# Short expert jobs on raw fp32 weights, and an fp32 gate, in a fused attention and mixture-of-experts kernel

## The chip, the cores and the metric

The kernel runs on one core of a Trainium2 chip. The metric is the device time of one launch, in microseconds; lower is better. Engines are named as in the profile: PE is the matrix engine (TensorE; PEld its weight loads), DVE the vector engine, ACT the scalar engine, POOL GpSimd, SP the engine that issues most DMAs.

## The reference

Three parts follow one another: an attention over 1152 tokens (2 batches of 512 local and 64 global rows, 8 heads of 64), a dense expert layer, and a layer that sends each token to one of 8 experts. The change concerns the third, and the gate in front of it:

```
logits = x @ w_gate                       # x [1152, 512], w_gate [512, 8]
expert_idx = argmax(logits, axis=1)
gate_w = softmax(logits)[expert_idx]
# each expert takes its first 288 tokens, in order; the rest of them stay zero in the output
h = maximum(disp @ w1[e], 0)              # w1 [8, 512, 1024]
y = h @ w2[e]                             # w2 [8, 1024, 512]
out[i] = gate_w[i] * y[expert_idx[i], pos[i]]
```

All data is fp32. For the inputs that the reference makes, the experts get 197, 108, 0, 82, 696, 0, 5 and 0 tokens.

## The kernel before, in words

The attention and most of the dense layer fill the first 180 us. Then the dense layer's output product is made in four windows of 256, 288, 256 and 288 token columns (`moe_second`, L689). Products that need fp32 accuracy are made from splits: a value is stored as a rounded fp32r part and the fp32r remainder, and three fp32r products (high by high, high by low, low by high) stand for one.

**The gate.** For each window, `moe_second` copies each of four 128-row chunks of x out of PSUM (ACT, L714), splits it (DVE, L715 and L716), and multiplies both halves by `wgs`, in which the gate's weights and their remainders stand side by side, padded to 128 columns (two products a chunk, L699: a pair). `gate_weights` (L637) makes `wgs` once. `tail_logits` (L728) copies the 16 rows of the result, `lt`, to SBUF (L734, or L1090 for the last window), and small products with `dup8` (`ptl`, L738) turn them over and add the two halves; the copies to `L` (L740) begin the routing. For window 3, the last pair stands outside the loop, behind the transposes of job 0's last tokens (`xp`, L803), and ahead of job 0's first layer.

**The jobs.** The experts are ranked by count; job 0 is the largest, and empty ones come last. `first_wide` and `second` run job 0; while they do, `final` (L1101) and what it calls compute the routing of all tokens and the tile `order` (L1140), which holds each job's expert and count. Jobs 1 to 8 are each a `unit` of 128 tokens (`job`, L981), with two more units under branches (L988, L990) for jobs above 128 and 256. A unit costs the same for any number of tokens up to 128. First layer (L887): tokens are stationary, the weights move, 512 columns at a time, 24 products; relu to `hs` (L892), transposes (L908) and splits to `hhl` (L909, L910); second layer (L921), 24 products; scaling by the gate's value (L927) and an indirect DMA that scatters the rows to the output (L928). Beside it run, at places given by step counts: the splits of the next job's raw weights (`split`, ACT L828 and DVE L829), each followed by the load of the job after that into the raw buffer (L822, L824; from job 2 on under a condition, the count); the gather of tokens (L791) and their transposes and splits (`xprep`, L799). Raw weights stand in eight buffers of 128x1024 (`raw2`). The jobs are nested: behind each job a branch on the next count (L1164) goes on or jumps past all the code that is left.

**What sets the order.** `drive` (L760) runs a main generator, one step per product, and starts its sides when their step is due: a side's `yield n` means that its next piece comes n steps later. The pieces stand in that order in each engine's program; an engine works its program in order, and waits on others by semaphores.

## Time and profile before

| | us |
|---|---|
| median of 3 runs (345.7 to 345.88) | 345.73 |
| the profiled execution | 347.64 |
| its span, first to last instruction | 345.86 |
| attention, dense layer, windows 0 to 3 (to the start of job 0's first layer) | 239.8 |
| job 0, first and second layer | 239.8 to 272.4 |
| job 1 (two units) | 272.4 to 298.7 |
| job 2 | 298.7 to 311.8 |
| job 3 | 311.8 to 324.9 |
| job 4 | 324.9 to 338.4 |
| landing of the last output and closing | 338.4 to 345.9 |

PE is busy 325.7 us, 94% of the span; DVE 73%, ACT 54%, POOL 41%. The mean granted clock of PE is 0.98. Times in a timeline count from the span's start. In a row, the number behind `x` is how many instructions were put together, and square brackets hold the idle time of that engine just before and who ended it; matmul records overlap, so the pace is read from the next start and not from their length.

### The profile page before, as it was taken

How to read it: one execution, taken by the hardware profiler on the slowest of the kernel's cores; microseconds unless marked ns; L12 is line 12 of the kernel's file. 1: busy time of each engine (PE TensorE's matmuls, PEld its weight loads, DVE VectorE, ACT ScalarE, POOL GpSimd, SP SyncE). 2: the span in 40 equal slices, each digit the busy share in tenths (PEclk: the TensorE clock that was granted, in tenths of full speed). 3: DMA queues.
4: the chain of work that ended last, by engine and by line, in shares of the span. 5: the costliest groups of instructions: out<-in, count | busy, mean ns of one | idle time of the engine just before them, and what ended most of it. 6: DMA issues, size and time to landing. Idle time of an engine off the chain costs nothing. (4 is left out here: it accounts for less than half of the span.)

```text
span 345.9 us, 8542 instructions
## 1 busy us (share of the span) xinstructions
PE 325.7 (94%) x3119; PEld 271.1 (78%) x3119; DVE 251.0 (73%) x662; ACT 185.1 (54%) x461; POOL 141.5 (41%) x168
## 2 busy tenths in 40 slices
PE   7989779999998999999999999999999999999990
PEld 2444547777787899999999999998987778777780
DVE  1777979985879448998993327867997893387881
ACT  3975666866675232423441223355525892488890
POOL 0375678664557517757784000310005542111211
PEclk9998987999999999999999999999999999999998
DMA  7975669490427913133300033665397999187100
GB/s 244 411 258 205 218 227 329 167 336 12 148 110 210 185 55 123 67 117 123 122 2 0 2 121 137 215 214 193 127 395 261 341 323 341 62 293 252 53 30 15
DMA packets 26293, 60.91 MB, mean 176 GB/s; under 512 B 3019, under 2 KB 8139, under 8 KB 26240
## 3 DMA queue, kind: packets, MB, share of 16 engines
q1 hardware_dynamic: 24640, 55.69, 46.8%
q0 software_dynamic: 1600, 4.54, 4.1%
q8 instruction: 30, 0.49, 0.6%
q14 instruction: 23, 0.19, 0.2%
HBM read 61.64 MB, written 7.47 MB: 200 GB/s over the span
## 5 line engine op out<-in xcount | busy, mean ns | idle before, releaser
L426 PE MATMUL h<-xh,wh 128*128 128x256 f32 (+1 forms) x288 | 84.6, 294 | 0.4 <-DVE hA L413 0.4
L426 PE MATMUL h<-xl,wh 128*128 128x256 f32 (+1 forms) x288 | 84.7, 294 | 0.0
L426 PE MATMUL h<-xh,wl 128*128 128x256 f32 (+1 forms) x288 | 84.3, 293 | 0.0
L426 PEld LDWEIGHTS h<-xl,wh 128*128 128x128 f32 x288 | 55.1, 191 | 0.9 <-issue 0.7
L426 PEld LDWEIGHTS h<-xh,wh 128*128 128x128 f32 x288 | 54.9, 191 | 1.1 <-DVE hA L413 0.6
L426 PEld LDWEIGHTS h<-xh,wl 128*128 128x128 f32 x288 | 55.0, 191 | 0.3 <-issue 0.2
L416 POOL TENSOR_TENSOR hTl<-hA,hTh 128x256 fp32r<-128x256 f32 (+1 forms) x24 | 19.3, 802 | 58.0 <-ACT hTh L415 57.1
L791 POOL DMA_INDIRECT xg<-x2d,idsall x12 | 14.6, 1220 | 60.8 <-DMA rawb<-in_w_dram 33.3
L829 DVE TENSOR_TENSOR w1l<-rawb,w1h 128x1024 fp32r<-128x1024 f32 x20 | 24.0, 1226 | 11.6 <-ACT w1h L828 11.6
L921 PE MATMUL py<-w2h,hhl 128*128 128x512 f32 x112 | 29.7, 395 | 0.0
L415 ACT CAST hTh<-hA 128x256 fp32r<-128x256 f32 (+1 forms) x24 | 10.0, 418 | 35.2 <-DVE hA L413 35.2
L829 DVE TENSOR_TENSOR w2l<-rawb,w2h 128x1024 fp32r<-128x1024 f32 x23 | 27.4, 1218 | 1.9 <-ACT w2h L828 1.8
L226 POOL CAST xh<-xs 128x128 fp32r<-128x128 f32 x32 | 13.1, 409 | 37.7 <-ACT xs L224 37.7
L708 PE MATMUL x<-hTl,wo_h 128*128 128x256 f32 (+1 forms) x96 | 28.2, 294 | 0.0
L708 PE MATMUL x<-hTh,wo_l 128*128 128x256 f32 (+1 forms) x96 | 27.9, 291 | 0.2 <-POOL wo_l L328 0.2
L708 PE MATMUL x<-hTh,wo_h 128*128 128x256 f32 (+1 forms) x96 | 27.8, 290 | 0.0
L188 ACT ACTIVATE sm<-sm,nm 128x128 f32<-128x128 f32 x64 | 25.2, 399 | 4.7 <-DVE nm L183 4.6
L327 POOL TENSOR_TENSOR ct<-ct,wh 128x512 f32<-128x512 f32 x18 | 25.6, 1420 | 1.5 <-DVE ca L324 1.5
L413 DVE TENSOR_TENSOR hA<-hA,h 128x256 f32<-128x256 f32 (+1 forms) x48 | 20.7, 431 | 7.2 <-PE h L426 6.5
L328 POOL TENSOR_TENSOR wl<-ct,ca 128x512 fp32r<-128x512 f32 x18 | 23.9, 1329 | 2.9 <-DVE ca L326 1.6
L921 PEld LDWEIGHTS py<-w2h,hhl 128*128 128x128 f32 x112 | 20.9, 188 | 4.5
L183 DVE CUSTOM_DVE_ANT_0 sm<-s,mask 128x128 f32<-128x128 f32 x64 | 15.9, 285 | 10.4 <-PE s L171 10.0
(213 smaller groups left out, 767.3 us busy)
## 6 DMA issues: line engine op xcount, KB each, us to landing
rawb<-in_w_dram SPq DMA_DIRECT2D x51, 512.0 KB
raww<-in_w_dram SPq DMA_DIRECT2D x18, 512.0 KB
rawv<-in_v_dram SPq DMA_DIRECT2D x16, 512.0 KB
qk<-in_qk_dram SPq DMA_DIRECT2D x16, 320.0 KB
rawo<-in_w_out_dram SPq DMA_DIRECT2D x6, 512.0 KB
rw<-in_w_dram SPq DMA_DIRECT2D x5, 512.0 KB
out_dram<-zero SPq DMA_DIRECT2D x1, 2176.0 KB
rawg<-in_vo_dram SPq DMA_DIRECT2D x4, 512.0 KB
```

Source lines behind the costliest of these rows:

```text
L183: nc.vector.tensor_tensor_reduce(sm[:, j], ps[:, j, 0:P], mk, scale=-0.125, scalar=3.0e38, op0=ALU.add, op1=ALU.min, accum_out=nm[:, j : j ...
L188: nc.scalar.activation(sm[:, j], sm[:, j], AF.Exp, bias=nm[:, j : j + 1], scale=-1.0, accum_out=ssum[:, j : j + 1])
L226: nc.gpsimd.tensor_copy(dst[0], xs)
L327: nc.gpsimd.tensor_tensor(tf, tf, hi.bitcast(F32), op=ALU.subtract)
L328: nc.gpsimd.tensor_tensor(lo, tf, b.bitcast(F32), op=ALU.add)
L413: nc.vector.tensor_tensor(hA[:, :T], hA[:, :T], ph[:, :T], op=ALU.max)
L416: nc.gpsimd.tensor_tensor(hl[:, f_, c0 : c0 + T], hA[:, :T], dst.bitcast(F32), op=ALU.subtract)
L426: nc.tensor.matmul(ph[:, :T], lhsT=w_[:, a], rhs=x_[:, c, c0 : c0 + T], start=n == 0, stop=n == 11)
L708: nc.tensor.matmul(po[:, :T], lhsT=w_[:, f, d * P : (d + 1) * P], rhs=h_[:, f_, c0 : c0 + T], start=k == 0, stop=k == 17)
L791: nc.gpsimd.indirect_dma_start(out=xg[t], out_offset=None, in_=src, in_offset=bass.IndirectOffsetOnAxis(ap=IDS[j][0:n, t, 0:1].bitcast(I32 ...
L829: nc.vector.tensor_tensor(l_, raw_of(j, k), h_.bitcast(F32), op=ALU.subtract)
L921: nc.tensor.matmul(py[0:nt], lhsT=a[:, c, a0 : a0 + nt], rhs=w_[:, c], start=i == 0, stop=i == 23)
```

## The change

There are two parts. **Small jobs.** From job 2 on, a job of at most 32 tokens runs through `small` (L979 on). It takes the tokens unsplit (`XS`, a copy of 32 columns that `xprep` now makes) and the raw fp32 weights out of the eight raw buffers. In the first layer, 32 token columns are stationary and a quarter of the 1024 hidden columns moves in each of four column groups of PE: 4 x 4 products of 256 columns into one PSUM tile, groups in turn. Relu is shared by ACT and DVE, two transposes make the hidden part stationary, and the second layer is 2 x 4 x 4 products of 128 columns, a quarter of the output columns in each group. Four scalings put the quarters beside one another in `ys`. The branch between jobs now compares with 32, then with 0; the code of `small` stands first and the longer job's in the Else. Since the small job's weights are not split, what follows one isn't loaded by the usual path: `order` gets two more rows, the counts by which loads are done, and what is left over; jobs left over run in `rest`, at the end, one after the other. With the counts above, only job 4 is small, and nothing is left over. Job 3 still makes the splits of job 4's weights and its split tokens.

**Gate.** The gate's products are fp32 by fp32 in the same form: `wg` is padded to 32 columns, chunk d of x goes to column group d, four products a window in place of eight, and the four partial sums are added by the `dup8` product, which now contracts over 128 rows. The splits of x, `wgs`, `gate_weights` and the products inside the loop go. In window 3 the products move into `first_wide`, at its step 5, and `ptl` follows 8 steps later.

```diff
@@ -112,7 +112,7 @@
     ident = cst[:, 0:P]
-    dup8 = cst[0:16, 256:264]
+    dup8 = cst[:, 256:264]
@@ -134,6 +134,8 @@
     ones_b = const.tile([P, P], BF16, name="ones_b")
+    wg = const.tile([P, 4, 32], F32, name="wg")
+    nc.gpsimd.memset(wg, 0.0)
...
     def routing_start():
@@ -630,14 +632,7 @@
-    wg = s2.tile([P, 4, NE], F32, name="wg")
-    nc.sync.dma_start(wg, w_gate.rearrange("(c p) e -> p c e", p=P))
-    wgs = s2.tile([P, 4, P], F32R, name="wgs")
-    def gate_weights():
-        nc.vector.tensor_copy(wgs, zero.unsqueeze(1).to_broadcast([P, 4, P]))
-        nc.vector.tensor_copy(wgs[:, :, 0:NE], wg)
-        nc.vector.tensor_tensor(wgs[:, :, NE : 2 * NE], wg, wgs[:, :, 0:NE].bitcast(F32), op=ALU.subtract)
+    nc.sync.dma_start(wg[:, :, 0:NE], w_gate.rearrange("(c p) e -> p c e", p=P))
@@ -648,8 +643,6 @@
                     take(ws, 1)
-                if k == 100:
-                    gate_weights()
@@ -663,15 +656,13 @@
                 s2b.tile([P, 4, 288], F32, tag="x2T", name=f"x2T{wi}"),
-                [s2b.tile([P, 288], F32R, tag="x2hl", bufs=4, name=f"x2hl{wi}{i}") for i in range(4)],
-                s2b.tile([16, 288], F32, tag="lt", name=f"lt{wi}"),
+                s2b.tile([P, 288], F32, tag="lt", name=f"lt{wi}"),
...
             rawb[:, a : a + 288 * 4].rearrange("p (d c) -> p d c", d=4),
-            x2hl,
-            rawb[0:16, 288 * (8 + wi - 2) : 288 * (9 + wi - 2)],
+            rawb[:, 288 * (8 + wi - 2) : 288 * (9 + wi - 2)],
@@ -691,13 +682,6 @@
         x2T = XB[wi][0]
-        pl_ = ps_y.tile([P, 512], F32, tag="py", name=f"pl{c0}")
-        x2 = {}
-        def logits(d):
-            for k, x_ in enumerate(x2[d]):
-                nc.tensor.matmul(pl_[:, :T], lhsT=wgs[:, d], rhs=x_[:, :T], start=d == 0 and k == 0, stop=d == 3 and k == 1)
@@ -709,15 +693,9 @@
                         yield
-            x2h, x2l = XB[wi][1][2 * (d % 2) : 2 * (d % 2) + 2]
-            x2[d] = (x2h, x2l)
             nc.scalar.copy(x2T[:, d, :T], po[:, :T])
-            nc.vector.tensor_copy(x2h[:, :T], x2T[:, d, :T])
-            nc.vector.tensor_tensor(x2l[:, :T], x2T[:, d, :T], x2h[:, :T].bitcast(F32), op=ALU.subtract)
-            if d:
-                logits(d - 1)
             yield
-        TAIL.append((c0, T, x2T, pl_, logits))
+        TAIL.append((c0, T, x2T))
@@ -727,11 +705,12 @@
     def tail_logits(wi):
-        c0, T, x2T, pl_, logits = TAIL[wi]
-        lt = XB[wi][2]
-        if wi < 3:
-            logits(3)
-            nc.vector.tensor_copy(lt[:, :T], pl_[0:16, :T])
+        c0, T, x2T = TAIL[wi]
+        lt = XB[wi][1]
+        pl_ = ps_y.tile([P, 512], F32, tag="py", name=f"pl{c0}")
+        for d in range(4):
+            nc.tensor.matmul(pl_[32 * d : 32 * d + 32, :T], lhsT=wg[:, d], rhs=x2T[:, d, :T], start=True, stop=True)
+        nc.vector.tensor_copy(lt[:, :T], pl_[:, :T])
@@ -741,12 +720,12 @@
     def tail_rows(wi):
-        c0, T, x2T, pl_, logits = TAIL[wi]
+        c0, T, x2T = TAIL[wi]
...
                 nc.tensor.transpose(pt[0:n, d], x2T[:, d, c - c0 : c - c0 + n], ident)
-            xs = XB[wi][3][i]
+            xs = XB[wi][2][i]
@@ -804,6 +783,10 @@
         nc.vector.tensor_tensor(l_, pt[:, :, 0:nt], h_.bitcast(F32), op=ALU.subtract)
+        if j > 1 and t == 0:
+            nc.vector.tensor_copy(XS[0], pt[:, :, 0:32])
+    XS = []
     def hl_of(j, k):
@@ -814,10 +797,11 @@
-    def load(j, k):
+    def load(j, k, kw=None):
         if j < NJ:
-            kw = {} if j < 2 else {"cond": nsp[j] > 0}
+            if kw is None:
+                kw = {} if j < 2 else {"cond": nsp[j] > 0}
@@ -990,11 +974,70 @@
+    SMALL = 32
+    def small(j):
+        sx = pB.tile([P, 512], F32, tag="hs", bufs=2, name="sx")
+        sh = pB.tile([P, 512], F32, tag="hs", bufs=2, name="sh")
+        xs = XS[0]
+        ph = ACC[0][0]
+        for k in range(4):
+            for g in range(4):
+                r = slice(32 * g, 32 * g + 32)
+                nc.tensor.matmul(ph[r, 0:256], lhsT=xs[:, k], rhs=raw_of(j, k)[:, 256 * g : 256 * g + 256], start=k == 0, stop=k == 3)
+        hr = sx[:, P : P + 256]
+        hT_ = sh[:, 0:256].rearrange("p (i t) -> p i t", i=2)
+        pt = ps_x.tile([P, 2, P], F32, tag="px", name="st")
+        for i in range(2):
+            s_ = slice(i * P, i * P + P)
+            if i == 0:
+                nc.scalar.activation(hr[:, s_], ph[:, s_], AF.Relu)
+            else:
+                nc.vector.tensor_scalar_max(hr[:, s_], ph[:, s_], 0.0)
+        for i in range(2):
+            nc.tensor.transpose(pt[:, i], hr[:, i * P : i * P + P], ident)
+            if i == 0:
+                nc.scalar.copy(hT_[:, i], pt[:, i])
+            else:
+                nc.vector.tensor_copy(hT_[:, i], pt[:, i])
+        py = ps_y.tile([P, P], F32, tag="py", name="sy")
+        for i in range(2):
+            for k in range(4):
+                for q in range(4):
+                    r = slice(32 * q, 32 * q + 32)
+                    nc.tensor.matmul(py[r], lhsT=hT_[:, i, 32 * k : 32 * k + 32], rhs=raw_of(j, 4 + k)[:, i, q * P : q * P + P], start=i == 0 and k == 0, stop=i == 1 and k == 3)
+        i_ = IDS[j][0:32, 0]
+        y = pB.tile([P, DM], F32, tag="y", bufs=2, name="ys")
+        for q in range(4):
+            if q:
+                nc.scalar.mul(y[0:32, q * P : q * P + P], py[32 * q : 32 * q + 32], i_[:, 2:3])
+            else:
+                nc.vector.tensor_scalar(y[0:32, 0:P], py[0:32], i_[:, 2:3], None, op0=ALU.mult)
+        nc.gpsimd.indirect_dma_start(
+            out=out, out_offset=bass.IndirectOffsetOnAxis(ap=i_[:, 1:2].bitcast(I32), axis=0),
+            in_=y[0:32], in_offset=None, bounds_check=NT - 1, oob_is_err=False)
+    def value(i, j, top, **kw):
+        _, (r,) = nc.values_load_multi_w_load_instructions(order[0:1, i, j - 1 : j], min_val=0, max_val=top, **kw)
+        return r
+    def rest():
+        for j in range(3, NJ):
+            with tc.If(value(3, j, NT) > 0):
+                ereg[j] = value(0, j, NE - 1, engines=(mybir.EngineType.SP,))
+                for k in range(8):
+                    load(j, k, {})
+                gather_tile(j, 0)
+                xprep(j, 0, ps_x, "px")
+                small(j)
...
     wv0 = rt.tile([P, 1, NE], F32, name="wv0")
-    ereg, nreg, nsp = [None] * NJ, [None] * NJ, [None] * NJ
+    ereg, nreg, nsp, nrest = [None] * NJ, [None] * NJ, [None] * NJ, [None] * NJ
...
     def early():
@@ -1045,7 +1088,6 @@
     raw2 = [rawb[:, i * F2 : (i + 1) * F2] for i in range(NR)]
-    x2hl = [pA.tile([P, 288], F32R, name=f"x2hl{i}") for i in range(4)]
@@ -1086,23 +1128,23 @@
     )
-    TAIL[3][4](3)
-    nc.vector.tensor_copy(XB[3][2], TAIL[3][3][0:16, :288])
...
     xT[1] = pB.tile([P, 2, 4, CAP], F32R, name="xT1")
-    order = rt.tile([P, 2, NE], I32, name="order")
-    Y0, Y1, Y2, Y3, Y4 = 10, 12, 44, 12, 3
+    XS.append(pB.tile([P, 4, 32], F32, name="x32"))
+    order = rt.tile([P, 4, NE], I32, name="order")
+    Y0, Y1, Y2, Y3, Y4 = 10, 12, 40, 12, 3
     def final():
...
         rows_1(As[0], columns(0, 5), 5)
+        yield 4
@@ -1133,10 +1175,14 @@
         nc.vector.tensor_tensor(g_, r_.unsqueeze(1).to_broadcast([P, NE, NE]), eidx.unsqueeze(2).to_broadcast([P, NE, NE]), op=ALU.is_equal)
-        o_ = rt.tile([P, 2, NE], F32, tag="ordf", name="ordf")
+        o_ = rt.tile([P, 4, NE], F32, tag="ordf", name="ordf")
...
             nc.vector.tensor_reduce(o_[:, i], p_, axis=AX.X, op=ALU.add)
+        nc.vector.tensor_copy(o_[:, 2, 0:2], o_[:, 1, 0:2])
+        nc.vector.scalar_tensor_tensor(o_[:, 2, 2:NE], o_[:, 1, 1 : NE - 1], float(SMALL), o_[:, 1, 2:NE], op0=ALU.is_gt, op1=ALU.mult)
+        nc.vector.tensor_tensor(o_[:, 3], o_[:, 1], o_[:, 2], op=ALU.subtract)
+        nc.vector.tensor_reduce(o_[:, 3, 0:1], o_[:, 3, 2:NE], axis=AX.X, op=ALU.max)
@@ -1144,7 +1190,7 @@
         if a < b:
-            for i, (to, top) in enumerate(((ereg, NE - 1), (nsp, NT))):
+            for i, to, top in ((0, ereg, NE - 1), (2, nsp, NT)):
...
     def count_of(j):
@@ -1161,7 +1207,10 @@
         if j + 1 < NJ:
-            with tc.If(nreg[j + 1] > 0) if j > 1 else ExitStack():
+            with tc.If(nreg[j + 1] <= SMALL) as c:
+                with tc.If(nreg[j + 1] > 0):
+                    small(j + 1)
+            with c.Else():
@@ -1171,7 +1220,10 @@
     accumulators()
+    more_ = value(3, 1, NT)
     jobs(1)
+    with tc.If(more_ > 0, preferred_fallthrough_block=False):
+        rest()
@@ -1225,7 +1277,7 @@
     dup = np.zeros((P, NE))
-    dup[np.arange(16), np.arange(16) % 8] = 1.0
+    dup[np.arange(P), np.arange(P) % 32 % NE] = np.arange(P) % 32 < NE
```

In PE's program, where window 3 ends and `first_wide` begins (`xp` transposes job 0's last tokens, `ph` is `first_wide`'s first layer, `px` and `ptl` belong to the gate's tail). Before:

```order
L708 MATMUL x_3800<-hTh_2506,wo_l 128x288
L699 MATMUL pl_3698<-x2hl_3519,wgs 128x288
L699 MATMUL pl_3698<-x2hl_3520,wgs 128x288
L803 MATMUL xp_3838<-cst,xg_3525 128x32 x4
L699 MATMUL pl_3698<-x2hl_3521,wgs 128x288
L699 MATMUL pl_3698<-x2hl_3522,wgs 128x288
L866 MATMUL ph<-xT_3526,w1h_3527 128x288 x4
L866 MATMUL ph<-xT_3526,w1l_3528 128x288 x3
L748 MATMUL px_3883<-cst,rawb 32x128 x4
L866 MATMUL ph<-xT_3526,w1l_3528 128x288
L866 MATMUL ph<-xT_3526,w1h_3527 128x288
L738 MATMUL ptl_3892<-cst,rawb 32x8
```

The last pair stands between `xp` and `ph`, and `ptl` behind nine products of `ph`. In PE's program after the change, the same place:

```order
L692 MATMUL x_3738<-hTh_2508,wo_l 128x288
L782 MATMUL xp_3772<-cst,xg_3486 128x32 x4
L850 MATMUL ph<-xT_3487,w1h_3488 128x288 x4
L850 MATMUL ph<-xT_3487,w1l_3489 128x288
L712 MATMUL pl_3813<-rawb,wg 32x288 x4
L850 MATMUL ph<-xT_3487,w1l_3489 128x288 x2
L727 MATMUL px_3821<-cst,rawb 32x128 x4
L850 MATMUL ph<-xT_3487,w1l_3489 128x288
L850 MATMUL ph<-xT_3487,w1h_3488 128x288 x5
L717 MATMUL ptl_3838<-cst,rawb 32x8
```

No pair is left, the four fp32 products stand behind five products of `ph`, and `ptl` behind thirteen.

In DVE's program, the same place (`pct` to `col_all` and `sc` are routing, `w2l` a split of job 0's weights, `L` the copy of `ptl`). Before:

```order
L716 TENSOR_TENSOR x2hl_3522<-rawb,x2hl_3521 128x288
L806 TENSOR_TENSOR xT_3526<-xp_3838,xT_3526 128x4x32
L1090 COPY rawb<-pl_3698 16x288
L486 TENSOR_SCALAR pct<-pos_all 128x5
L487 SCALAR_TENSOR_TENSOR pct<-pos_all,pct 128x5
L488 SCALAR_TENSOR_TENSOR pcm<-pct,pos_all 128x5
L490 TENSOR_SCALAR col_all<-pos_all 128x5
L491 TENSOR_TENSOR col_all<-col_all,pct 128x5
L496 TENSOR_TENSOR sc_3864<-iota_b,pcm 128x640
L829 TENSOR_TENSOR w2l_3530<-rawb,w2h_3529 128x1024
L740 COPY L<-ptl_3892 32x8
```

The copy of the logits (`rawb<-pl`) comes first, ahead of the routing and the split. In DVE's program after the change, the same place:

```order
L785 TENSOR_TENSOR xT_3487<-xp_3772,xT_3487 128x4x32
L488 TENSOR_SCALAR pct<-pos_all 128x5
L489 SCALAR_TENSOR_TENSOR pct<-pos_all,pct 128x5
L490 SCALAR_TENSOR_TENSOR pcm<-pct,pos_all 128x5
L492 TENSOR_SCALAR col_all<-pos_all 128x5
L493 TENSOR_TENSOR col_all<-col_all,pct 128x5
L498 TENSOR_TENSOR sc_3796<-iota_b,pcm 128x640
L813 TENSOR_TENSOR w2l_3491<-rawb,w2h_3490 128x1024
L713 COPY rawb<-pl_3813 128x288
L855 SCALAR_TENSOR_TENSOR hhl<-ph,hhl 128x256
L857 SCALAR_TENSOR_TENSOR hhl<-ph,hhl 128x32
L719 COPY L<-ptl_3838 32x8
```

The copy now stands behind the split, and a piece of `first_wide`'s hidden layer (`hhl`) ahead of `L`.

In PE's program, from job 3 to job 4 (`acc` is a unit's first layer; `st` and `sy` are the transposes and the second layer of `small`). Before:

```order
L921 MATMUL py<-w2l_3858,hhl 32x512 x4
L921 MATMUL py<-w2h_3857,hhl 32x512 x4
L990 UNCONDITIONAL_BRANCH x2
L988 UNCONDITIONAL_BRANCH
L1164 COMPARE_AND_BRANCH
L887 MATMUL acc_4349<-w1h_3527,xT_3526 128x512 x4
L887 MATMUL acc_4349<-w1l_3528,xT_3526 128x512 x3
```

The longer job's first layer follows the branch directly. In PE's program after the change, the same place:

```order
L905 MATMUL py<-w2l_3789,hhl 32x512 x4
L905 MATMUL py<-w2h_3788,hhl 32x512 x4
L974 UNCONDITIONAL_BRANCH x2
L972 UNCONDITIONAL_BRANCH
L1210 COMPARE_AND_BRANCH
L1211 COMPARE_AND_BRANCH
L988 MATMUL acc_4291<-rawb,x_3791 32x256 x16
L999 MATMUL st<-cst,sx 128x128 x2
L1009 MATMUL sy<-rawb,sh 32x128 x32
L1211 UNCONDITIONAL_BRANCH x2
L871 MATMUL acc_4291<-w1h_3488,xT_3487 128x512 x4
```

The 50 products of `small` stand between the branch and the longer job, which a longer job jumps over; the same stands from job 1 to 2 and from job 2 to 3.

## Rows read from the trace of the kernel before

**Rows 1.** Busy us by stage: window, length, five engines, granted clock, DMA share, GB/s.

```profile
238.20:255.60 17.40, 17.00 (x135) 15.80 (x134) 15.55 (x61) 7.92 (x16) 0.00 (x0) 1.00 0.51 181
...
272.40:285.90 13.50, 13.50 (x70) 10.62 (x69) 13.06 (x16) 12.57 (x18) 6.55 (x6) 1.00 0.96 350
...
324.85:338.44 13.59, 12.80 (x60) 10.03 (x60) 11.79 (x12) 11.57 (x15) 2.34 (x2) 1.00 0.11 35
338.44:345.90 7.46, 0.00 (x0) 0.00 (x0) 0.44 (x1) 0.00 (x0) 1.05 (x1) 0.77 0.05 12
```

**Rows 2.** Timeline of the last job: start, duration, engine, line, operation, shapes, idle time before.

```profile
324.86 1.19 PE L887 MATMUL acc<-w1h,xT 128*128 128x512 f32 x4 [0.32 <-PEq L988]
...
325.60 1.12 POOL L928 DMA_INDIRECT out_dram<-y,idsall  x1 [3.44 <-ACTq L988]
...
336.57 1.09 PE L921 MATMUL py<-w2h,hhl 128*128 128x512 f32 x4
337.75 0.69 ACT L927 ACTIVATE y<-py,idsall 128x512 f32<-128x512 f32 x1 [0.59 <-ACT w2h L828]
338.71 1.05 POOL L928 DMA_INDIRECT out_dram<-y,idsall  x1 [3.52 <-ACTq L988]
```

**Rows 3.** Timeline, TensorE in the attention: fp32 products, one at a time, then in column groups.

```profile
31.27 0.75 PE L240 MATMUL sgp<-qk,qg 128*64 128x320 f32 x2
...
61.22 0.43 PE L213 MATMUL pv<-rawv,ph 128*32 128x64 f32 x16
...
69.96 0.65 PE L277 MATMUL gpv<-rawg,gph 128*32 128x64 f32 x32
```

**Rows 4.** Landing of output writes: the one issued at 325.60, then all five together.

```profile
DMA to landing us min/median/max: 4.3/4.3/4.3
...
DMA to landing us min/median/max: 2.6/4.3/7.8
```

**Rows 5.** Timeline, TensorE: a pair of gate products in window 0, and what follows it.

```profile
189.30 0.40 PE L699 MATMUL pl<-x2hl,wgs 128*128 128x256 f32 x2
189.53 0.28 PE L708 MATMUL x<-hTh,wo_h 128*128 128x256 f32 x1
```

**Rows 6.** Timeline, end of window 3 and start of job 0, TensorE, VectorE and ScalarE.

```profile
238.20 0.42 PE L699 MATMUL pl<-x2hl,wgs 128*128 128x288 f32 x2
...
238.55 0.43 PE L803 MATMUL xp<-cst,xg 32*128 32x32 f32 x4
...
239.02 0.27 ACT L805 CAST xT<-xp 128x128 fp32r<-128x128 f32 x1 [0.22 <-PE xp L803]
...
239.20 0.89 PE L699 MATMUL pl<-x2hl,wgs 128*128 128x288 f32 x2 [0.21 <-DVE x2hl L715]
239.55 0.28 DVE L806 TENSOR_TENSOR xT<-xp,xT 128x128 fp32r<-128x128 f32 x1
...
239.80 0.59 PEld L866 LDWEIGHTS ph<-xT,w1h 128*128 128x128 f32 x4
...
240.13 0.45 DVE L1090 COPY rawb<-pl 16x288 f32<-16x288 f32 x1 [0.29 <-PE pl L699]
...
241.64 0.76 PE L738 MATMUL ptl<-cst,rawb 16*32 16x8 f32 x6
241.98 1.22 DVE L829 TENSOR_TENSOR w2l<-rawb,w2h 128x1024 fp32r<-128x1024 f32 x1
```

**Rows 7.** Timeline, VectorE: the cast of the job order, and the splits behind it.

```profile
259.96 0.42 DVE L1140 CAST order<-ordf 128x16 int32<-128x16 f32 x1
...
263.67 3.53 DVE L829 TENSOR_TENSOR w1l<-rawb,w1h 128x1024 fp32r<-128x1024 f32 x3 [2.40 <-ACT w1h L828]
```

**Rows 8.** Jumps over two units (L988) on TensorE: count, ns min/median/max, starts.

```profile
L988 PEldq COMPARE_BRANCH  x3: 313/318/318, 308.8 to 334.9; - x3
```

**Rows 9.** Branches of L1164 to the next job on TensorE, and ScalarE's last waits, same columns.

```profile
L1164 PEldq COMPARE_BRANCH  x4: 70/132/3445, 311.7 to 341.7; - x4
...
L1164 ACTq EVENT_SEMAPHORE  x2: 17/17/17, 341.3 to 341.4; - x2
```

## The prediction

> **What bounds the kernel now.** I read the busy times by stage first, then the timeline of the last job, then the timeline where the gate's last window meets job 0. In the stages of job 0 and of job 1's first unit, TensorE is busy 17.0 of 17.4 and 13.5 of 13.5 us at a granted clock of 1.00, its upper level, 2.4 GHz [rows 1]; so a product removed there shortens the chain and a wait added to TensorE lengthens it. The reference's inputs put 197, 108, 0, 82, 696, 0, 5 and 0 tokens on the experts: jobs of 288 (capped), 197, 108, 82 and 5 tokens. Only the last, job 4, is at most 32. It takes a whole job's 13.59 us [rows 1] for 5 tokens: TensorE from 324.86, the scaling at 337.75, the output write at 338.71, then 7.15 us of landing and closing to 345.86 with no engine at work [rows 2]. What moves that write's issue moves the end.
>
> **Job 4, products.** The changed form multiplies fp32 by fp32 with 32 stationary columns. One fp32 product is two records; of the one with 320 columns the two take 0.75 us and one alone 0.48 on average, so a pass costs 0.27 us, 0.84 ns a column, and about 0.22 us to drain [rows 3]. In four column groups 16 records of 64 columns take 0.43 and 32 take 0.65 [rows 3]: 16 more cost 0.22, where 16 x 64 x 0.84 ns one after another is 0.86. The four groups run at once. The Trainium skill, "TensorE: Matmul & The Clock Gate", section "Part 3: Packing small matmuls — row/col tiling", speaks against a full factor: 3.07 times with four row tiles, 2.38 with three column tiles; as an estimate at 3.07 the new products would cost 1.6 us more and the time would be 340.3. These rows say four, though no row shows it at 128 or 256 columns, so the row decides for the forecast.
>
> The first layer is 32 records of 256 columns: 32 x 256 x 0.84 ns / 4 + 0.22 = 1.94 us. The second is 64 of 128 columns, 1.94 too. Between them stand relu, two transposes and a copy. ScalarE and VectorE take 0.27 and 0.28 for 128x128 out of PSUM; four small transposes take 0.43 [rows 6], so two are taken as 0.3. With 0.15 of handing over that is 1.0 us. Two branches that are not taken stand where one did, at 0.07 [rows 9]. So TensorE starts at 324.95, ends layer one at 326.9, starts layer two at 327.9 and is done at 329.85.
>
> **Job 4, output.** The new y is the buffer of job 3's y, whose write was issued at 325.60 [rows 2] and landed 4.3 us later [rows 4], at 329.9: a tie. Three scalings on ScalarE at 0.27 give 330.75. The write follows a scaling's end by 0.27 (337.75 + 0.69 to 338.71) [rows 2], so it is issued at 331.05, **7.66 us earlier**. Landing and closing follow as before. But TensorE's jump over the unused jobs, which takes 3.45 us now [rows 9], is followed by one over the code for what is left over: 329.9 + 3.45 + 0.1 + 3.45 = 336.9. ScalarE's last wait stands at 341.3, 2.9 us after its scaling [rows 2, 9], so twice that gives 336.6. The closing needs them by about 337.2, hence both stay hidden; POOL's own extra jump I put at **+0.3** (0 to 2). Removed with job 4's old form are ScalarE's and VectorE's splits for an empty job 5; nothing waits for them.
>
> **Gate.** A pair of gate products occupies 0.23 us to the next start [rows 5]: four are 0.94 in a window of 256 and 1.05 in one of 288. Four fp32 products in column groups are 0.43 us of passes plus part of the drain, 0.55 (0.43 to 0.65), or 0.62 at 288. Windows 0 to 2 gain 0.39 + 0.43 + 0.39 = 1.2. Window 3 loses two pairs on the chain, 0.53; the third hides under the wait for job 0's tokens. The last pair, which waited for VectorE's split, goes: first_wide's loads start at 239.80 [rows 6], and without it when ScalarE's copy is done, 239.02 + 0.27, so 0.45 earlier. Against that, the products come back inside first_wide at 0.62. And ptl, 9 steps into first_wide now, stands at step 13; its input, the lt copy, stands on VectorE behind xT, five small ops, sc and a whole split of 1.22 (in the trace: 240.13 for the copy, the split at 241.98 behind it) [rows 6]. That stretch moves 0.6 earlier, so the split ends about 242.4 and the copy (0.45) at 242.85, while TensorE arrives about 242.1: a stall with the hand-over of 0.85 (0 to 1.2). Behind the wait are first_wide's own products. Sum: -1.2 - 0.53 - 0.45 + 0.62 + 0.85 = **-0.7** (-1.6 to +0.3). VectorE also drops the splits of x2; TensorE was not waiting for those of windows 0 to 2.
>
> **Order of the jobs.** VectorE gets four small ops before the cast to order, each at most that cast's 0.42: at most 1.7, and 2.40 us of idle time stand a few rows later [rows 7]. The weight loads of job 2 go out that much later ahead of a stage where DMA is 0.96 busy [rows 1]; I take 0 and keep 0.5. The copy of 32 columns per job to XS is at most the 0.28 of a 128x128 one; in job 1's first unit VectorE has 13.06 of 13.5 us filled [rows 1], in the others more room: nothing, at most 0.3. One more register load, once: +0.1 (0 to 0.3).
>
> **Branches.** From job 1 to 2 and from 2 to 3 the branch falls through now, 0.07 us [rows 9], and will be taken, over small's code. TensorE's jump over two units takes 0.32 [rows 8]; small has 50 products, the two units 112, so this is the nearest row, and the far end is the 3.45 of the last jump [rows 9]. I take 0.45 each, since it stands directly behind a jump of the other kind: **+0.9** with the extra compare (0.2 to 6.9).
>
> **Sum.** -7.66 + 0.3 - 0.7 + 0.1 + 0.9 = -7.0 us in a span of 345.86. The profiled execution took 347.64; the median of the runs is 345.73, and the difference carries over: **338.7 us**.
>
> **Rivals.** *Jumps into code that is not there.* For it: the last jump's 3.45 [rows 9]; against it: 0.32 three times [rows 8]. One of the two at 3.45 gives 341.7, both 344.7, and with a closing that TensorE's second far jump prolongs by up to 2 us, 346.7. The Trainium skill, "Runtime: NRT & Kernel Launch", section "Instruction fetch mechanics", says that a taken branch out of the two pages held waits for a fetch; by that the 3.45 is a far target, and the new jumps depend on where a page ends.
>
> *Job 3's write lands late.* All five landings reach from 2.6 to 7.8 us [rows 4]. At 7.8 the scaling waits until 333.4 instead of 329.9: 342.2.
>
> *The gate goes to an end of its range.* No gain: 339.4; no stall at ptl: 337.8.
>
> *The groups overlap in part.* From the shorter row with its drain, 0.86 / 0.43 = 2.0 [rows 3]. Serial, job 4's products are 13.7 us and the gate's 7.3; at 2.0 this costs 3.0 and 1.3 us more than taken: 343.0.
>
> *The groups do not overlap at these widths* (slower than before). Then job 4 costs 10.2 and the gate 5.0 us more: 354. It turns to slower below an overlap of 21 / (5.25 + 7.0) = 1.7. Against it stand both rows of four groups.
>
> *The change doesn't do what it says*: the fourth count is above 32 and the branches alone stay: -0.7 + 0.1 + 1.4 + 0.1, 346.6. Against it: five units of output after job 0, and the 5 tokens.
>
> **How the numbers follow.** Forecast 0.60; one far jump 0.09; both 0.05 (of it 0.02 faster, 0.02 same, 0.01 slower); late landing 0.08; gate 0.08; part overlap 0.05; no overlap 0.03; no small job 0.02. Faster by over 0.2% (0.7 us, about what a measurement of this kernel can tell from no change): 0.92, same 0.02, slower 0.06. The low end is the forecast with the gate at -1.6, branches at 0.2 and no extra jump of POOL: 336.8. The high end takes in the landing and one far jump: 342.2.
>
> **What would show it.** In job 4: the first layer's records (L988 of the changed kernel) in under 2.1 us and the second's (L1009) too, the scaling starting at once, or idle with the earlier write as its cause; the write at about 7 us ahead of the old. In first_wide: an idle stretch of TensorE ahead of ptl with the lt copy as releaser. At 1 to 2 and 2 to 3: branches on TensorE of 0.3 rather than 3 us. After the last write: closing of some 7.4 us. The prediction is wrong if TensorE's gaps between jobs grow by over 1 us each, or if the groups' records follow one another.

## The result, and the profile after

The changed kernel takes 343.01 us (median of 22 runs, against 346.95 for 22 runs of the kernel before); the ratio is 0.988, 95% interval 0.986 to 0.991. Two of its runs, at 346.28 and 432.46 us, were over 1.5% above its fastest, and the ratio leaves them out. The changed kernel is 3.9 us faster where 7.0 were forecast, and its median lies outside the range of 336.8 to 342.2. The forecast started from 345.73, and the kernel before takes 1.2 us more in these runs; on the forecast's base the gain gives 341.8. The profiled execution has a span of 342.68 us.

Spans don't compare well here: the attention, whose code is nearly the same in all these kernels, ended up to 3.3 us apart from one profiled execution to the next (first product of window 0 at 179.4 to 182.7 us). So I compare from that product on, stage by stage, each from its first TensorE product to that of the next (differences of starts in the timelines; the last two stages are cut at the issue of the last output write). The columns to the right are experiments told of below.

| stage, us | before | after | gate only | shifted back | no rest |
|---|---|---|---|---|---|
| windows 0 to 3 | 57.78 | 54.54 | 54.58 | 54.54 | 54.54 |
| job 0, first layer | 15.67 | 16.23 | 16.23 | 16.24 | 16.32 |
| job 0, second layer | 16.87 | 17.09 | 16.87 | 17.06 | 16.81 |
| job 1, first unit | 13.68 | 13.69 | 13.68 | 13.67 | 13.72 |
| job 1, second unit, to job 2 | 12.56 | 12.84 | 12.56 | 12.96 | 12.96 |
| job 2, to job 3 | 13.13 | 16.41 | 13.13 | 13.28 | 13.28 |
| job 3, to job 4 | 13.03 | 14.76 | 13.03 | 13.31 | 13.31 |
| job 4, to the issue of its output | 13.85 | 7.20 | 13.85 | 7.20 | 7.22 |
| landing and closing | 7.15 | 7.27 | 7.31 | 8.45 | 4.00 |
| sum | 163.7 | 160.0 | 161.2 | 156.7 | 152.2 |

Two things moved by more than they should, in opposite directions: the windows gained 3.2 us, and jobs 2 and 3 lost 5.0 between them.

**Between jobs 2 and 3.** TensorE's three branches to the next job in the kernel after (count, ns as min/median/max, first and last start), the answer to [rows 9]:

```profile
L1210 PEldq COMPARE_BRANCH  x3: 72/219/3350, 296.8 to 327.8; - x3
```

The one from job 1 to 2 takes 0.22 us, the one from 3 to 4, not taken, 0.07; the one from 2 to 3 takes 3.35. The timeline of TensorE there:

```profile
308.76 1.10 PE L905 MATMUL py<-w2h,hhl 128*128 128x512 f32 x4
313.45 2.07 PE L871 MATMUL acc<-w1h,xT 128*128 128x512 f32 x4 [3.60 <-ACT w1h L812]
315.32 1.73 PE L871 MATMUL acc<-w1l,xT 128*128 128x512 f32 x4
```

The last group of job 2 starts at 308.76 and its products end at 309.85; job 3 starts 3.60 later. The row blames ScalarE's w1h, whose last split for job 3 had ended at 303.77:

```profile
302.72 1.05 ACT L812 CAST w1h<-rawb 128x1024 fp32r<-128x1024 f32 x1
```

And job 3's first products come slowly: four take 1.87 to the next start, where the same four of job 2 take 1.04. The busy times (columns as in [rows 1]) of job 2's first products and of job 3's:

```profile
297.04:300.20 3.16, 3.16 (x14) 2.58 (x15) 1.57 (x2) 2.02 (x4) 1.00 (x1) 1.00 0.14 50
313.45:317.82 4.37, 4.37 (x13) 3.48 (x13) 0.94 (x1) 0.00 (x0) 0.00 (x0) 0.63 0.88 335
```

Behind the 3.6 us of idling, TensorE's granted clock is 0.63 on average over 4.37 us, between its two levels of 1.2 and 2.4 GHz; job 2's stretch ran at 1.00. Job 3's thirteenth product from its start is followed after 4.60 us, job 2's after 3.12: 1.5 us lost.

**The gate's place.** The timeline that answers to [rows 6]:

```profile
236.87 0.27 ACT L784 CAST xT<-xp 128x128 fp32r<-128x128 f32 x1
...
237.19 0.79 PE L850 MATMUL ph<-xT,w1h 128*128 128x288 f32 x4 [0.35 <-ACT xT L784]
...
238.04 0.69 PE L712 MATMUL pl<-rawb,wg 128*32 128x288 f32 x8
...
238.66 0.54 PE L850 MATMUL ph<-xT,w1l 128*128 128x288 f32 x2
238.87 1.22 DVE L813 TENSOR_TENSOR w2l<-rawb,w2h 128x1024 fp32r<-128x1024 f32 x1
...
240.00 0.45 DVE L713 COPY rawb<-pl 128x288 f32<-128x288 f32 x1
...
240.51 0.68 PEld L717 LDWEIGHTS ptl<-cst,rawb 128*32 128x32 f32 x6 [0.31 <-DVE rawb L713]
```

job 0's first layer starts 0.05 after ScalarE's copy; the four fp32 products take 0.62 to the next start; the copy of the logits starts behind the split, and ptl's weights wait 0.31 us for it.

**Job 4**, answering to [rows 2]:

```profile
328.21 1.93 PE L988 MATMUL acc<-rawb,x 128*32 128x256 f32 x32 [0.56 <-DVE w2l L813]
...
330.29 0.28 ACT L995 ACTIVATE sx<-acc 128x128 f32<-128x128 f32 x1 [1.86 <-PE acc L988]
...
330.62 0.33 PE L999 MATMUL st<-cst,sx 128*128 128x128 f32 x1 [0.47 <-ACT sx L995]
330.67 0.29 DVE L997 TENSOR_SCALAR sx<-acc 128x128 f32<-128x128 f32 x1 [1.52 <-ACT sx L995]
330.98 0.27 ACT L1001 COPY sh<-st 128x128 f32<-128x128 f32 x1 [0.42 <-PE st L999]
...
331.30 0.33 PE L999 MATMUL st<-cst,sx 128*128 128x128 f32 x1 [0.36 <-ACT sh L1001]
...
331.56 1.95 PE L1009 MATMUL sy<-rawb,sh 128*32 128x128 f32 x64
...
333.58 0.34 DVE L1016 TENSOR_SCALAR ys<-sy,idsall 32x128 f32<-32x128 f32 x1 [1.62 <-PE sy L1009]
334.00 1.14 ACT L1014 ACTIVATE ys<-sy,idsall 32x128 f32<-32x128 f32 x3 [2.76 <-DVE ys L1016]
335.42 0.89 POOL L1017 DMA_INDIRECT out_dram<-ys,idsall  x1 [5.39 <-POOLq L1210]
```

The two layers take 1.93 and 1.95 us. In between, VectorE's relu starts when ScalarE's has ended, and the second transpose when ScalarE's copy has; ScalarE's scalings start when VectorE's has ended. The write goes out 7.20 us after the start, in place of 13.85.

### The profile page after: what moved, and what is told of

Its sections match the earlier page's. It is cut to its first block, busy times and chain, and to the rows that moved or that the text cites. A ratio compares the mean times of both kernels' runs of the same rounds, so it can differ in the third digit from the quotient of the medians.

```text
span 342.7 us, 8538 instructions
## 1 busy us (share of the span) xinstructions
PE 315.9 (92%) x3157; PEld 260.5 (76%) x3157; DVE 229.0 (67%) x626; ACT 175.7 (51%) x452; POOL 140.0 (41%) x168
## 3 DMA queue, kind: packets, MB, share of 16 engines
HBM read 57.19 MB, written 7.27 MB: 188 GB/s over the span
## 5 line engine op out<-in xcount | busy, mean ns | idle before, releaser
L770 POOL DMA_INDIRECT xg<-x2d,idsall x11 | 12.6, 1144 | 57.4 <-DMA rawb<-in_w_dram 31.0
L813 DVE TENSOR_TENSOR w1l<-rawb,w1h 128x1024 fp32r<-128x1024 f32 x16 | 19.1, 1223 | 14.2 <-ACT w1h L812 14.0
L905 PE MATMUL py<-w2h,hhl 128*128 128x512 f32 x96 | 25.5, 395 | 0.0
L813 DVE TENSOR_TENSOR w2l<-rawb,w2h 128x1024 fp32r<-128x1024 f32 x19 | 22.7, 1219 | 1.8 <-ACT w2h L812 1.8
L871 PE MATMUL acc<-w1h,xT 128*128 128x512 f32 x64 | 18.0, 415 | 4.5 <-ACT w1h L812 3.6
```

What stands on the lines that cost most here:

```text
L813: nc.vector.tensor_tensor(l_, raw_of(j, k), h_.bitcast(F32), op=ALU.subtract)
L871: nc.tensor.matmul(ph[0:nt], lhsT=a[:, c], rhs=w_[:, c, sl], start=i == 0, stop=i == 11)
L905: nc.tensor.matmul(py[0:nt], lhsT=a[:, c, a0 : a0 + nt], rhs=w_[:, c], start=i == 0, stop=i == 23)
```

## Experiments

The theory (A): the branch from job 2 to 3 waits for TensorE's next code, and its place decides. The rival (B): TensorE waits for ScalarE's split, as the row names it.

**Shifted back by 4 KB.**

```diff
+pairs = ((xh_, w1h), (xh_, w1l), (xl_, w1h))[: 1 if (j, t) == (1, 2) else 3]
-for a, w_ in ((xh_, w1h), (xh_, w1l), (xl_, w1h)):
+for a, w_ in pairs:
...   and the same in second(): two products in three left out of a unit that is never entered
```

> Edit: in job 1's third unit, which the data never enters, two products in three are left out, so TensorE's program behind it stands 4 KB earlier; nothing that runs is changed (a job 1 of over 256 tokens would come out inexact). Theory A (TensorE's taken branch over the small job's code, from job 2 to 3, waits for the code to be fetched, because that branch crosses from one block of fetched code to the next right after another jump did; the branch took 3.35 us): shifted so that branch and target stand in one block, the branch takes 0.2 to 0.4 us, job 3 starts without the pause, its first layer runs at clock 1.00 and not 0.63, and the time is 4.4 to 5 us below the changed kernel: ratio to before about 0.975, span about 338. Theory B (TensorE waits there for ScalarE's first split w1h, as the profile names the releaser): nothing changes, span 342.5, the idle 3.6 us ahead of job 3 stay.

Measured: ratio 0.985 (0.980 to 0.989), 339.84 us. The branches to the next job:

```profile
L1212 PEldq COMPARE_BRANCH  x3: 72/224/353, 293.4 to 320.0; - x3
```

and the jumps over two units ahead of them (from job 2's and 3's first unit), with job 2's last products, then the same jumps in the changed kernel (and job 1's), then the busy times of job 2's and job 3's first products:

```profile
L974 PEldq COMPARE_BRANCH  x2: 715/1108/1502, 303.9 to 317.2; - x2
...
305.54 1.10 PE L907 MATMUL py<-w2h,hhl 128*128 128x512 f32 x4
```

```profile
L972 PEldq COMPARE_BRANCH  x3: 95/328/337, 281.5 to 325.0; - x3
```

```profile
293.83:297.00 3.17, 3.17 (x14) 2.59 (x15) 1.70 (x2) 2.02 (x3) 1.00 (x1) 1.00 0.14 50
307.11:310.30 3.19, 3.19 (x14) 2.61 (x15) 2.48 (x3) 2.27 (x4) 1.31 (x1) 1.00 0.84 227
```

The branch from 2 to 3 takes 0.22 and the clock stays at 1.00; jobs 2 and 3 take 13.28 and 13.31. ScalarE's and VectorE's work is unchanged, so B falls. The wait has not gone: the jump ahead takes 1.50 in place of 0.34 us. But that jump, from 303.9 to 305.4, stands while products of job 2 are still in TensorE's queue, until 306.6, and costs nothing. By the stages 4.6 us of jobs 2 and 3 come back, and 1.2 go again at the end (8.45 in place of 7.27 us), which the section on the kernel without rest takes up. The time fell less than A had it: 0.975 was expected, and in the same rounds it is 3.0 us below the kernel shifted on by 5 KB (342.87), which keeps the stall, not 4.4 to 5.

**Shifted on by 5 KB.**

```diff
 with tc.If(nreg[j] > 2 * P):
+    for _ in range(40 if j == 1 else 0):
+        nc.tensor.matmul(ACC[1][0][0:32], lhsT=xT[1][:, 0, 0, 256:288], rhs=WS[1][0][:, 0, 0:512], start=True, stop=True)
     unit(j, 2, ...)
```

> Edit: 40 products are added in job 1's third unit, which is never entered, so TensorE's program behind it stands 5 KB later; nothing that runs is changed. Theory A: the branch from job 2 to 3 keeps its 3.3 us, and the one from job 1 to 2 now crosses into a block that is not there yet right behind the jump over the unit, and takes 3 us too, with a lower clock behind it: 3 to 5 us above the changed kernel, span 346 to 348, no faster than before. Theory B: span 342.5 and a branch of 0.2 us from job 1 to 2.

Measured: ratio 0.986 (0.982 to 0.989), 342.87 us: as the changed kernel. Branches, and TensorE's first products of job 3:

```profile
L1212 PEldq COMPARE_BRANCH  x3: 72/423/2787, 296.2 to 327.0; - x3
```

```profile
312.53 2.03 PE L871 MATMUL acc<-w1h,xT 128*128 128x512 f32 x4 [3.04 <-ACT w1h L812]
```

The stall of 2.8 us and the slow start stay, as A has it, and the row's blame of ScalarE with it. The second stall, from job 1 to 2, did not come (0.42), and with it the 3 to 5 us more that I expected. My map of which code is loaded when is right for the one place and wrong for the other.

**Shifted on by 12 KB** (the same edit with 96 products).

> Edit: 96 products in job 1's third unit, which is never entered, so TensorE's program behind it stands 12 KB later than in the changed kernel. Theory A (the branch from job 2 to 3 waits for code): if the code comes in blocks of 16 KB, 12 KB later is the same place in a block as 4 KB earlier, where the branch took 0.22 us: so again 0.2 to 0.5 us from job 2 to 3, job 3 starts 13.2 us after job 2 and works at clock 1.00, time 3.5 to 5 us below the changed kernel (about 339.5). If what counted in the first shift was the shorter program and not the place, the branch takes 3 us again as it did 5 KB later.

Measured: ratio 0.977 (0.970 to 0.984), 339.01 us. Branches:

```profile
L1212 PEldq COMPARE_BRANCH  x3: 72/221/427, 294.0 to 320.7; - x3
```

0.22 from job 2 to 3 again, with a longer program. What counts is the place of the branch in the program. The Trainium skill, "Runtime: NRT & Kernel Launch", section "Instruction fetch mechanics", gives blocks of 16 KiB, 256 instructions, and a fetch at a taken branch that leaves the code held. A product is two instructions, a load of weights and a multiplication, so by these figures 32 products less and 96 more are the same place in a block, and the KB of the shifts are estimates worked out from them. At this branch the three shifts agree with the Trainium skill: 0.22, 0.22 and 2.79 us, against 3.35 unshifted.

**The fetch in the traces.** Code comes by DMA, in packets of a queue of its own. The profile's page of the changed kernel has (queue, packets, MB, share)

```profile
q8 instruction: 33, 0.54, 0.7%
```

which is 16 KB a packet. From 283 us on, the twelve traces hold 30 branches of TensorE that take over 0.6 us. Every one ends 1.3 to 1.6 us, once 2.0, after such a packet is in. Those with one packet that starts after the branch does take 2.8 to 3.8 us: the stall above runs from 310.05 to 313.39, its packet from 311.05 to 312.02. Those with two take 4.4 to 5.5, all of them at the end. Those whose packet had started before take 0.7 to 3.0: the jump shifted back runs from 303.92 to 305.42, its packet from 303.02 to 304.11. Of the shorter branches one alone has a packet in it. So the stall is a wait for code, seen and not only inferred from the shifts.

**Small code only from job 4 on.**

```diff
 if j + 1 < NJ:
+    if j < 3:
+        with tc.If(nreg[j + 1] > 0) if j > 1 else ExitStack():
+            jobs(j + 1)
+        return
     with tc.If(nreg[j + 1] <= SMALL) as c:
```

> Edit: the code of the small job stands only behind job 3 and later; jobs 2 and 3 follow by the old branch (a job 2 or 3 of at most 32 tokens would run as a whole one, which these counts don't have). Theory A: the two taken branches are gone, TensorE's branches to jobs 2 and 3 take 0.1 us, no pause ahead of job 3, clock 1.00: 4.8 to 5.3 us below the changed kernel, span 337.5. If a taken branch of the short kind costs more than its own length, it is below the shifted kernel by more than 0.5. Theory B: idle 3.6 us ahead of job 3 as now, span 342.5.

Measured: ratio 0.982 (0.978 to 0.985), 340.01 us. TensorE at the start of jobs 3 and 4:

```profile
309.24 1.18 PE L871 MATMUL acc<-w1h,xT 128*128 128x512 f32 x4 [0.32 <-PEq L972]
...
322.54 2.65 PE L988 MATMUL acc<-rawb,x 128*32 128x256 f32 x32 [0.57 <-DVE w2l L813]
```

0.32 us of idling ahead of job 3 as before the change, and no slow start: A again. By the stages it is 3.7 us below the changed kernel, where 4.8 to 5.3 were expected, and no better than the shifted ones: job 4's first layer takes 2.65 in place of 1.93 at a clock of 1.00, with a pause inside, and landing and closing take 8.1. The pause ends at 323.27, 1.4 us after a packet of code is in at 321.88, which is the pattern of the branches; no run moves it.

**The gate alone.** The hunks of small, rest, XS, order and the branches are undone.

> Edit: the fp32 gate stays, small jobs are taken out (all jobs by the old path, old branches, old job order). By the trace of the changed kernel, job 1's second unit starts 1.7 us earlier than before, so the gate alone is expected at 1.7 us below before (ratio 0.995, span 344.1); by my prediction's sum 0.7 (ratio 0.998, span 345.2). If the earlier start is given back in jobs 1 to 4 (loads or splits that don't come earlier), less than 1.

Measured: ratio 0.992 (0.989 to 0.994): 2.8 us less, more than both numbers. TensorE's branches are those of before again:

```profile
L1204 PEldq COMPARE_BRANCH  x4: 70/132/3759, 308.1 to 338.4; - x4
```

The stages tell where: 3.20 gained in the windows, 0.56 lost in job 0's first layer, and from there to the last write's issue each stage as before within 0.01. So the losses between the jobs belong to the other part of the change.

**gate_weights back, on the gate alone.**

```diff
+if k == 100:
+    nc.vector.tensor_copy(wz, zero...)
+    nc.vector.tensor_copy(wz[:, :, 0:NE], wg[:, :, 0:NE])
+    nc.vector.tensor_tensor(wz[:, :, NE : 2 * NE], wg[:, :, 0:NE], wz[:, :, 0:NE].bitcast(F32), op=ALU.subtract)
```

> Edit: to the kernel with the fp32 gate alone, VectorE's three operations of gate_weights (1.8 us at 151 to 153 us before) are put back at their old place, on a tile that nothing reads. Theory: they delay the last split of w_out (POOL), on which TensorE waited 0.4 us in window 0 before; the wait comes back and window 0 takes 9.0 us in place of 8.6. Rival (the wait went for another reason): window 0 stays at 8.6.

In the one execution of this kernel, window 0 takes 9.02 us (8.62 without), and TensorE waits for POOL in it again:

```profile
182.78 0.39 PE L697 MATMUL x<-hTh,wo_l 128*128 128x256 f32 x1 [0.16 <-POOL wo_l L330]
```

So 0.4 us of the gate's gain come from three VectorE operations 30 us earlier, which held up POOL's last split.

**No rest** (on the kernel shifted back).

```diff
-more_ = value(3, 1, NT)
 jobs(1)
-with tc.If(more_ > 0, preferred_fallthrough_block=False):
-    rest()
```

> Edit: on the kernel shifted back by 4 KB, the code for jobs left over and the branch around it at the end are taken out (with these counts it never runs). Theory: TensorE's two far jumps behind the small job, 4.85 and 4.71 us there, end after the output has landed and set the end; with one of them gone the time from the issue of the last output to the end falls from 8.45 to about 7.2 us, as before. Rival (landing and POOL's closing set the end): it stays at 8.4.

Measured: ratio 0.967 (0.960 to 0.973), 335.17 us; the end comes 4.00 us after the last write's issue, far below the 7.2 that I expected. The closing of the shifted kernel: its branches around rest, and the engines' last drains:

```profile
L1227 PEldq COMPARE_BRANCH  x2: 74/2390/4707, 330.0 to 330.4; - x2
...
L1227 POOLq INC_SWDGE_SEM  x1: 593/593/593, 330.6 to 330.6; - x1
```

```profile
L1311 POOLq DRAIN  x3: 46/107/1957, 331.7 to 335.8; - x3
...
L1311 PEldq DRAIN  x2: 8/36/65, 335.2 to 335.6; - x2
```

and the drains without rest:

```profile
L1308 POOLq DRAIN  x3: 46/107/1952, 329.2 to 331.7; - x3
...
L1308 PEldq DRAIN  x2: 8/40/73, 330.5 to 331.5; - x2
```

With rest, POOL waits at that branch until the output (issued at 327.62) has landed, counts (INC at 330.6) and starts its drain of 1.96 at 331.7; TensorE's second far jump of 4.71 us from 330.4 ends later still, and its drain at 335.2 is what the end follows. Without it, POOL's drain starts at 329.2, 1.2 us after the issue at 327.98 and ahead of the landing, and TensorE, one jump less, drains at 330.5. So this branch at the very end costs twice: a far jump, and a wait for landing that stood in series with POOL's drain. The kernel before has that series too.

**Groups one after the other** (on the kernel shifted back).

```diff
-for k in range(4):
-    for g in range(4):
+for g in range(4):
+    for k in range(4):
...   and the second layer with q outside
```

> Edit: on the kernel shifted back by 4 KB, the small job's products go through one column group after the other (groups in the outer loop), not through the groups in turn. Theory (the groups overlap because products for different groups stand next to one another): nearly serial, first layer 6 to 7 us in place of 1.93 and second layer the same, the last output 9 to 10 us later. Rival (the engine sorts them itself): 1.9 us as now; in between, TensorE looks ahead over some products.

```profile
322.75 4.57 PE L990 MATMUL acc<-rawb,x 128*32 128x256 f32 x32 [0.56 <-DVE w2l L813]
...
328.71 5.95 PE L1011 MATMUL sy<-rawb,sh 128*32 128x128 f32 x64
```

In the one execution of this kernel, 4.57 and 5.95 us in place of 1.93 and 1.95, the output 6.6 later, where 6 to 7 and 9 to 10 were expected. Most of the overlap comes from products of different groups standing next to one another; what is left of it (a serial count by the prediction's pace is 6.9 each) is more in the first layer, where a group changes every 8 records, and less in the second, every 16. The Trainium skill, "TensorE: Matmul & The Clock Gate", section "Part 3: Packing small matmuls — row/col tiling", measured 3.07 times with four row tiles and 2.38 with three column tiles. The four column groups here give 3.6 by the serial count, an estimate with the drain in the 1.93; no run is fully serial, and against this one they give 2.4 and 3.1.

**Own tiles for the halves** (on the kernel shifted on by 12 KB).

```diff
-hr = sx[:, P : P + 256]
-hT_ = sh[:, 0:256]...
+hr = (sx[:, P : 2 * P], sh[:, P : 2 * P])
+hT_ = (sx[:, 2 * P : 3 * P], sh[:, 2 * P : 3 * P])
+pts = [ps_x.tile([P, P], F32, tag="px", name=f"st{i}") for i in range(2)]
...   all four scalings on VectorE
```

> Edit: on the kernel shifted on by 12 KB, the small job's two halves get tiles of their own (ScalarE's relu and copy in one, VectorE's in the other, two PSUM tiles for the transposes), and VectorE does all four scalings. Theory (the two engines and TensorE wait for each other there because a tile is tracked as a whole): from first to second layer 1.0 us in place of 1.4, scalings 1.1 in place of 1.5, the last output issued 6.3 to 6.5 us after job 4's start in place of 7.24. Rival: the waits are between the operations themselves, 7.2. The end follows TensorE's far jumps, so the time falls by 0.4 to 0.8 against the shifted kernel: about 338.3.

```profile
324.98 0.28 ACT L997 ACTIVATE sx<-acc 128x128 f32<-128x128 f32 x1 [1.89 <-PE acc L990]
...
325.36 0.29 DVE L999 TENSOR_SCALAR sh<-acc 128x128 f32<-128x128 f32 x1 [1.59 <-ACT sx L997]
...
325.99 1.08 PE L1011 MATMUL sy<-rawb,sx 128*32 128x128 f32 x32
...
328.01 1.47 DVE L1015 TENSOR_SCALAR ys<-sy,idsall 32x128 f32<-32x128 f32 x4 [1.65 <-PE sy L1011]
329.76 0.88 POOL L1016 DMA_INDIRECT out_dram<-ys,idsall  x1 [5.11 <-POOLq L1209]
```

The output goes out after 6.88 in place of 7.24 us: under half of what I expected. The second layer starts 1.01 after ScalarE's relu in place of 1.27; but VectorE's relu still starts behind ScalarE's, which reads the same PSUM tile (whether that is why, no run shows), and four scalings on VectorE take 1.47, nearly the 1.56 of the mixed ones. The time, 340.03 (ratio 0.980, 0.975 to 0.984), can't be told from the shifted kernel's.

**Own tiles without rest** (shifted back).

> Edit: the same own tiles and scalings on the kernel without the code for jobs left over (shifted back by 4 KB). Theory: the output goes out 0.8 us earlier as there; behind it TensorE's one far jump of 5 us then ends later than POOL's closing, so 0.5 of it reaches the end: about 334.5 against 335.2, ratio to before 0.965. Rival (POOL's closing still ends last): the whole 0.8.

Measured: 335.43 us, ratio 0.966 (0.962 to 0.969), the same as without own tiles. The 0.34 at the output is there, but TensorE pauses in the middle of job 3:

```profile
311.86 0.86 PE L872 MATMUL acc<-w1l,xT 128*128 128x512 f32 x3
314.15 0.66 PE L893 MATMUL hp<-cst,hs 128*128 128x128 f32 x4 [1.43 <-issue]
```

TensorE starts these three products at 311.86 and its next work at 314.15, at a clock of 1.00, with 1.43 us of idling put down to nothing; job 3 takes 14.95 in place of 13.31. A packet of code is in at 312.53, 1.6 us before TensorE goes on, so late code is likely (the program's place moved again), though no run moves it back. The jump ahead of job 3 took 2.97 us, outlasted the queue, and costs job 2 another 0.27.

Without rest the time is 3.3% below that of the kernel before, and 2.3% below the changed one's (335.17 and 343.01). But the kernels shifted back come out inexact for a job 1 of over 256 tokens, and for counts that leave a second small job behind, rest's work would have to be put elsewhere. With everything kept, the kernel shifted on by 12 KB has the lowest time, 2.3% below the kernel before, though its interval overlaps those of the kernel shifted back, the one with own tiles and the one with small code from job 4 on.

## Why the prediction was wrong

- **Branches: the step that failed.** I took 0.45 us for each of the two taken branches, after a jump of about the same length, and gave 0.09 to the rival that one of them costs 3.45. The one from job 2 to 3 took 3.35, and job 2 with it 3.28 more than before (13.13 to 16.41). The length was the wrong likeness: what counts is whether the target is already loaded, and the trace of before showed only jumps whose target was there (0.32) and one that waited beside the landing of the output (3.45). The other branch cost 0.28, as taken or less.
- **The clock was left out of that rival.** A pause of 3.6 us is followed by 1.5 us of loss at a lower clock, which I had not priced; one far jump costs 3.28 + 1.46 = 4.7 more than the branch of before (1.46 against the same products shifted back), and not the 3.45 of that rival. On the forecast's base the measured time, 341.8, still meets the rival's 341.7, but by luck: the gate's extra 2.0 stand against the clock's 1.5 and the 1.3 by which job 4 gave less.
- **Gate: right in direction, the size wrong by 2.0.** -0.7 was taken, -2.7 measured (-3.2 in the windows, +0.56 after). The fp32 products cost what was worked out (0.57 and 0.62). In the windows the four that were missed add up to 1.06 over my 2.18: 0.46 of waiting for POOL in window 0 that hung on gate_weights, which the prediction does not have; 0.26 for window 3's third pair (from the last product of the window to xp 0.48 before, 0.22 after), which I had hidden under a wait for job 0's tokens, but those were there, and xp followed the pair after 0.35 [rows 6]; 0.14 more for the last pair (from xp to the first layer 1.38 before, 0.79 after); and 0.20 over the rest, where the products gave 0.3 less than I had and ptl gave 0.4. The rows of before for the first and the last of these:

```profile
184.53 0.39 PE L708 MATMUL x<-hTh,wo_l 128*128 128x256 f32 x1 [0.20 <-POOL wo_l L328]
184.75 0.28 PE L708 MATMUL x<-hTh,wo_h 128*128 128x256 f32 x1
...
228.89 0.61 PE L738 MATMUL ptl<-cst,rawb 16*128 16x8 f32 x4
229.42 0.40 PE L708 MATMUL x<-hTh,wo_h 128*128 128x288 f32 x1
```

  and of after for the last:

```profile
227.72 0.51 PE L717 MATMUL ptl<-cst,rawb 128*128 128x8 f32 x4
228.09 0.38 PE L692 MATMUL x<-hTh,wo_h 128*128 128x288 f32 x1
```

  ptl takes 0.37 to the next start in place of 0.53. In first_wide the stall at ptl is about 0.24 (0.37 between the starts around it, less 0.13 of pace), not 0.85: the products arrive 0.3 later than I had them, and the copy is 0.2 earlier.
- **Job 4, products: right.** 1.94 us forecast for each layer, 1.93 and 1.95 measured. Overlap in part, or none, fell.
- **Job 4, the chain between: mis-sized.** From layer to layer 1.42 us, not 1.0 (start of one to start of the other 3.35, less 1.93), and scalings 1.56 in place of 0.8: engines in turn where I had them side by side, and 0.38 for one scaling (1.14 for three) and not 0.27. Output 7.20 after the start, where 6.1 were forecast. The start itself came 0.28 later (job 3 takes 13.31 shifted back, 13.03 before), not 0.07, so job 4 gave 1.3 us less than taken.
- **Landing of job 3's write: no wait,** as taken. That write, issued at 328.70, landed 3.1 us later; the scaling started at 333.58, behind the last product, with 1.8 us to spare where I had a tie.
- **Closing: right by accident.** 7.27 for the 7.45 taken. But TensorE's second jump did not stay hidden by a margin: the answer to [rows 9] at the end is

```profile
L1225 PEldq COMPARE_BRANCH  x2: 74/2359/4644, 336.6 to 337.1; - x2
```

  and 337.1 + 4.64 ends at 341.7, level with POOL's drain (341.8); with the shift it ends last.
- **Order of the jobs: no price shown.** Job 0's second layer grew by 0.22, and by 0.19 shifted back; in both a pause of 0.2 that the profile puts down to nothing stands ahead of job 1. It is not the small operations or the load: the kernels shifted on, by 5 and by 12 KB, and the one with small code from job 4 on have them too, and take 16.81 there, less than the 16.87 of before. The cause stays open.

The sum by the measured terms: -2.7 gate, +0.2 in job 0's second layer, +0.3 and +3.3 and +1.7 between the jobs and in job 3, -6.65 for job 4, +0.1 at the end: -3.7 us in the trace, -3.9 in the runs.

## What to carry to other kernels

A branch's price is the price of its target: here 0.2 to 0.6 us where the code was there and 2.8 to 3.8 where a block had to come, and a few KB of dead code ahead of it decided over that. Move a taken branch under a queue of work. Look for idling that a trace puts down to an innocent engine, and then at the packets of the code itself. Price a pause of TensorE with the slow products that follow it. Many narrow fp32 products paid here when their column groups stood in turn (1.93 us against 4.57); then the short operations between them were the time.

## What I had not expected

- A branch around never-run code at the very end cost 4.45 us (8.45 to 4.00 from the last write's issue to the end), by a far jump of TensorE and by POOL's drain being put behind the landing.
- The attention's end scatters by 3.3 us between profiled executions at nearly the same code (window 0 starts at 179.4 to 182.7 us). TensorE's granted clock from 8 to 179 us goes with it: 1.00 where window 0 starts at 179.4 and 179.8, 0.99 at 180.1 to 181.7, 0.97 or 0.98 at 181.9 to 182.7. Why it falls in some executions and not in others, no run here shows.
- The far jumps of TensorE at the end took 3.3 to 5.5 us in these kernels, each with its own place.
